# More Strassen products at two levels in three down projections, with the chain's evictions moved from ScalarE and GpSimd to VectorE

## The chip, the cores and the metric

The kernel runs on one core of a Trainium2 chip. The metric is the device time of one execution in microseconds (us); lower is better. The engines are called by the profile's names: PE (TensorE, matmuls; PEld is its weight load), DVE (VectorE), ACT (ScalarE), POOL (GpSimd) and SP (SyncE, which issues the DMAs).

## The reference

Four blocks work on x (2048 tokens by 1024), each with a layernorm before it and a residual sum: a linear attention block (A), a gated bilinear block (B), A again, B again. The change touches B alone:

```python
def _B_ref(x, w_gate, w_up, w_down):
    g = jnp.einsum("bsd,df->bsf", x, w_gate)
    u = jnp.einsum("bsd,df->bsf", x, w_up)
    h = g * u
    return jnp.einsum("bsf,fd->bsd", h, w_down)
...
x = x + _B_ref(_layernorm(x, axis=-1), B_w_gate, B_w_up, B_w_down)
```

Here f is 3584, in 28 tiles of 128. Inputs and output are bf16.

## The kernel before

A B block (`layer_B`) runs over two halves of the tokens (`ps_` 0 and 1). For each half it makes h (`gateup`) and then multiplies it with w_down (`down`). So there are four down stages, called D1 to D4 here: D1 and D2 for the first B block (`first` true, halves 0 and 1), D3 and D4 for the second.

h is kept as four quarters `hA` to `hD` (two token blocks by two halves of f). A down stage uses Strassen's method in Winograd's form: seven products, in the order of `DPROD`, instead of eight. A product of one level is 4 token tiles of 14 matmuls of 128x512 (56). The products listed in `DTWO` are split once more (`two_level`): seven part products, each over 7 of f's tiles, in the order 1, 5, 6, 7, 2, 3, 4, each for p = 0 and 1, as 7 matmuls of 128x256 (98 in all). The part products are put together in PSUM: ACT copies (`seed`) and DVE adds (`join`) between the banks `tmp[p]` and the result banks `dst`. A part product writes to a bank only after the copies and adds that read it are through, since `_Prog.add` orders all accesses of one bank by different engines.

In D2, D3 and D4 (`chain`) products 1, 6 and 7 are summed in the same four PSUM banks: after product 1, after 6 and after 7 the running sum is taken out for each of the four token tiles t (`chain_step`): ACT copies it with a scale to a float32 buffer `rtmp` and POOL adds the residual tile x to it (`evict_x`, L2159 and L2161). Beside that, DVE makes the sums of h that later products need: in step 1 `e = a - d` and `a = c - e`, in step 6 `a = b - a` and `d = d + c`, each over 14 x 128 elements; and `a_sums` makes the four sums of blocks for the next two-level product (7 x 256 elements each), queued in `EX` and taken out one by one by `ex_pop`. The last of these tiles x are brought back from `x_scratch` by DMAs that `tail` issues in the middle of the first token tile of a down stage.

Each engine runs its own stream in the order in which the code calls `P.add`; `plan` turns the dependencies into semaphore waits. There is no scheduler beside it: what stands behind a waiting instruction on its engine waits too. Weights go through a ring of five slots (`ring_issue`); sums of weights for two-level products are made once in D1 (`r_sums`), stored to `d_scratch`, and loaded in D2 to D4. `x_pop` takes from a list of DVE operations that make the sums of x for the next gate and up stage.

L854 and L857 are the helpers `tt` (tensor plus or minus tensor) and `stt` (PSUM by a scale plus a tensor).

## Time and profile before

| | |
|---|---|
| median of 3 runs | 1426.22 us (1425.93 to 1427.45) |
| the profiled execution | 1425.98 us, of which the span is 1424.2 us |
| PE busy | 1419.1 us of the span, 8430 matmuls |
| DVE, ACT, POOL busy | 1167.1, 725.8, 291.1 us |
| D1, D2, D3, D4 | 399 to 483.5, 641 to 725, 1103 to 1184.5, 1342.5 to 1424.2 us |

The span is the time from the first to the last instruction that was recorded. The time of a run is 1.8 us longer than the span in the profiled execution. A busy PE may still have matmuls that follow each other at any pace; the count of matmuls beside the busy time tells the pace. The mean duration of a matmul includes the way through the array, which overlaps with the next one.

### The profile page before, as it was taken

The page shows a single profiled execution, that of the slowest core. Times are in us where ns is not written, and L with a number is a line of the kernel's source. Part 1 is how long each engine was busy: PE and PEld are TensorE (multiplying, and loading weights), DVE is VectorE, ACT ScalarE, POOL GpSimd, SP SyncE. Part 2 cuts the span into 40 slices and gives each one's busy share as a digit, 9 for nine tenths or more (in the row PEclk, how much of TensorE's full clock was granted, in tenths as well). Part 3 has the DMA queues.
Part 4 walks back from the last instruction along what each step waited for, and adds up shares of the span by engine and source line. Part 5 has one row for each costly group of instructions (what it writes and reads, how often), then busy time and mean ns, then how long its engine had stood idle before and what let it go on. Part 6 is the DMA issues. An engine that isn't in the chain of part 4 may idle for free.

```text
span 1424.2 us, 22547 instructions
## 1 busy us (share of the span) xinstructions
PE 1419.1 (100%) x8430; PEld 815.1 (57%) x8430; DVE 1167.1 (82%) x2040; ACT 725.8 (51%) x1529; POOL 291.1 (20%) x303
## 2 busy tenths in 40 slices
PE   9999999999999999999999999999999999999999
PEld 4444444555544655554864444456666477666658
DVE  7878788988878799778778878789877978777887
ACT  4752357667720355552256523557776115777521
POOL 4643632000000000004234346301000400000050
PEclk9999999999999999999999999999999999999999
DMA  7416767988977999996998067589975699778657
GB/s 238 110 23 197 173 139 196 319 285 271 326 249 252 313 270 294 296 255 221 311 335 215 27 180 171 127 230 269 287 257 197 231 319 299 257 259 260 214 189 258
DMA packets 362845, 331.73 MB, mean 233 GB/s; under 512 B 178544, under 2 KB 305776, under 8 KB 362224
## 3 DMA queue, kind: packets, MB, share of 16 engines
q1 hardware_dynamic: 362736, 330.29, 76.7%
q8 instruction: 66, 1.08, 0.3%
q14 instruction: 43, 0.35, 0.1%
HBM read 239.27 MB, written 67.37 MB: 215 GB/s over the span
## 4 chain that ended last, share of the span: by engine, by line
PE 99%; DVE 0%; DMA 0%; ACT 0%; issue 0%; POOL 0%
PE ps L1613 27%; PE ps L1692 18%; PE ps L2208 14%; PE ps L2100 9%; PE ps L1516 8%; PE ps L1414 8%; PE ps L1174 6%; PE ps L980 5%; PE ps L990 3%; PE ps L1428 1%; PE ps L1456 0%; DMA arena<-in_A_x_dram 0%; PE ps L612 0%; DVE arena L487 0%; PE ps L604 0%; PE ps L1440 0%
## 5 line engine op out<-in xcount | busy, mean ns | idle before, releaser
L854 DVE TENSOR_TENSOR arena<-arena 128x512 f16<-128x512 f16 (+9 forms) x784 | 473.5, 632 | 71.4 <-ACT arena L1736 41.2
L1613 PE MATMUL ps<-arena 128*128 128x512 f16 x1808 | 446.8, 380 | 0.0
L1692 PE MATMUL ps<-arena 128*128 128x256 f16 x2324 | 312.4, 273 | 0.7 <-ACT arena L1718 0.6
L857 DVE SCALAR_TENSOR_TENSOR arena<-ps,arena 128x512 f16<-128x512 f32 (+3 forms) x398 | 263.0, 682 | 40.0 <-PE ps L2208 17.9
L1692 PEld LDWEIGHTS ps<-arena 128*128 128x128 f16 (+1 forms) x2324 | 226.8, 98 | 102.1 <-DVE ps L1711 3.2
L1613 PEld LDWEIGHTS ps<-arena 128*128 128x128 f16 (+1 forms) x1808 | 176.8, 98 | 140.5 <-ACT ps L1643 0.3
L2208 PE MATMUL ps<-arena 128*128 128x512 f16 (+1 forms) x896 | 194.2, 380 | 0.0
L1618 ACT ACTIVATE arena<-ps 128x512 f16<-128x512 f32 x220 | 131.6, 598 | 93.1 <-PE ps L1613 91.2
L2161 POOL TENSOR_TENSOR arena<-arena 128x512 f32<-128x512 f32 x44 | 66.0, 1506 | 425.1 <-ACT arena L2159 340.6
L2208 PEld LDWEIGHTS ps<-arena 128*128 128x128 f16 x896 | 87.7, 98 | 105.3
L2100 PE MATMUL ps<-arena 128*128 128x256 f16 (+1 forms) x1176 | 130.1, 273 | 0.0
L2100 PEld LDWEIGHTS ps<-arena 128*128 128x128 f16 x1176 | 114.5, 98 | 14.9 <-DVE arena L857 0.2
L1711 DVE TENSOR_TENSOR ps<-ps,arena 128x256 f32<-128x256 f32 x220 | 92.3, 428 | 30.6 <-PE ps L1692 17.8
L1414 PE MATMUL ps<-arena 128*128 128x512 bf16 x512 | 115.4, 380 | 0.0
L490 POOL TENSOR_SCALAR arena<-arena 128x1 f32<-128x1 f32 x41 | 15.6, 379 | 486.7 <-DVE arena L489 486.7
L1516 PE MATMUL ps<-arena 128*128 128x512 bf16 x512 | 111.5, 380 | 0.0
L1708 ACT COPY ps<-ps 128x256 f32<-128x256 f32 x220 | 81.0, 368 | 48.3 <-PE ps L1692 42.7
L1174 PE MATMUL ps<-arena 128*128 128x512 bf16 (+1 forms) x420 | 94.9, 380 | 0.0
L1314 POOL TENSOR_TENSOR arena<-arena 128x1024 f16<-128x1024 f32 x32 | 80.2, 2506 | 66.4 <-DVE arena L1312 59.3
L1643 ACT COPY ps<-ps 128x512 f32<-128x512 f32 x112 | 64.3, 574 | 51.0 <-PE ps L1692 44.6
L1015 POOL TENSOR_TENSOR arena<-arena 128x512 f32<-128x512 f32 x60 | 73.6, 1245 | 72.2 <-DVE arena L1103 36.2
L1516 PEld LDWEIGHTS ps<-arena 128*128 128x128 f16 x512 | 50.1, 98 | 59.8
(83 smaller groups left out, 1275.5 us busy)
## 6 DMA issues: line engine op xcount, KB each, us to landing
arena<-w_scratch SPq DMA_DIRECT2D x84, 512.0 KB, 4.9
arena<-sp_scratch SPq DMA_DIRECT2D x56, 512.0 KB, 5.8
arena<-t_scratch SPq DMA_DIRECT2D x27, 896.0 KB, 5.7
arena<-in_B_w_down_dram SPq DMA_DIRECT2D x18, 896.0 KB, 6.6
w_scratch<-arena SPq DMA_DIRECT2D x28, 512.0 KB, 6.5
sp_scratch<-arena SPq DMA_DIRECT2D x28, 512.0 KB, 4.1
arena<-in_B_w_gate_dram SPq DMA_DIRECT2D x42, 256.0 KB, 5.0
arena<-in_B_w_up_dram SPq DMA_DIRECT2D x42, 256.0 KB, 3.2
```

Of the source, the lines that this page charges most:

```text
L854: P.add("dve", lambda e: e.tensor_tensor(out=out, in0=a, in1=b, op=op), rd=rd, wr=wr, prd=prd)
L857: P.add("dve", lambda e: e.scalar_tensor_tensor(out=out, in0=a, scalar=sc, in1=b, op0=ALU.mult, op1=op1), rd=rd, wr=wr, prd=prd)
L1174: P.add("pe", lambda e: [e.matmul(psb(bank), x[:, k, :], w[:, k, :], start=(start and k == 0), stop=(k == 3), skip_group_check=True) for k ...
L1414: return [e.matmul(psb(bank), xr[:, t, j * 128:(j + 1) * 128], pk[:, h, t, :], start=(t == tok[0]), stop=(t == tok[-1])) for t in ts]
L1516: return [e.matmul(psb(bank), xnT[:, g, i * 128:(i + 1) * 128], wp[:, g, dh * 512:(dh + 1) * 512], start=(dh == 0 and g == 0), stop=(g == ...
L1613: P.add("pe", lambda e: [e.matmul(psb(bank), w[:, k, :], x[:, k, :], start=(start and k == 0), stop=(k == 3), skip_group_check=True) for k ...
L1618: P.add("act", lambda e: e.activation(t, psb(bank), AF.Copy, scale=SG), prd=[bank], wr=r)
L1692: P.add("pe", lambda e: [e.matmul(psb(bank)[:, 256 * half:256 * half + 256], w[:, k, :], xx[:, k, :], start=(start and k == 0), stop=(k == ...
L1708: P.add("act", lambda e: e.copy(psb(dst[c])[:, 0:256], lo), prd=[bk], pwr=[dst[c]])
L1711: P.add("dve", lambda e: e.tensor_tensor(out=psb(dst[c])[:, 256:512], in0=lo, in1=c5, op=ALU.add), prd=[bk], rd=rc5, pwr=[dst[c]])
L2100: P.add("pe", lambda e: [e.matmul(psb(bank)[:, 256 * half:256 * half + 256], a[:, k, :], w[:, k, :], start=(start and k == 0), stop=(k == ...
L2208: return [e.matmul(psb(bank), hv[:, 7 * hf + k, t * 128:(t + 1) * 128], w[:, k, :], start=(start and hf == 0 and k == 0), stop=(hf == 1 an ...
```

## The change

Two-level products: D2 and D4 have five instead of four (7 is new), D3 has four instead of three (4 is new, and its order becomes that of D2 and D4). So 3 products of 56 matmuls become 3 of 98 half as wide.

In the chain, DVE now takes the running sum out of PSUM with one `stt` that adds x at once; the ACT copies and the POOL adds are gone. Where 7 is two-level, ACT copies the running sum after product 6 to `rtmp` 12 to 15, and the parts of product 7 are added to it by DVE (`ujoin`, `u5`, `ulow`), in place of `seed` and `join`. The sums of step 1 are made the other way round, and `d = d + c` is made in the gate and up stages, once for each of the 14 column blocks of a half. In D1 the sums of weights for 7 are added to the work of product 6 and stored. The `x_pop` calls move from the first products of D1 to its last, and are spread over D3 anew; the stores of x (`stash`) move from steps 6 and 7 to 1 and 6.

```diff
-        L2D = "5324"
-        DPROD = {(True, 0): "1267453", (True, 1): "1672453", (False, 0): "1674253", (False, 1): "1672453"}
-        DTWO = {(True, 0): "", (True, 1): L2D, (False, 0): "532", (False, 1): L2D}
+        L2D = "53247"
+        DPROD = {(True, 0): "1267453", (True, 1): "1672453", (False, 0): "1672453", (False, 1): "1672453"}
+        DTWO = {(True, 0): "", (True, 1): "53247", (False, 0): "5324", (False, 1): "53247"}
...
                 def fmul(q, c):
...
+                    if c and q in "43":
+                        made.append(q)
+                        if len(made) == 2:
+                            j = units[0]["j"]
+                            rc_, rd_ = [R(H[i][1] + j * 1024, 1024) for i in "43"]
+                            tt(hD[:, j, :], hD[:, j, :], hC[:, j, :], ALU.add, rd_ + rc_, rd_)
...
+                def evict7(t, bank):
+                    evict_x(12 + t, bank, xq(1, 0, t))
+                    evict_x(8 + t, bank, xq(1, 1, t))
...
+                    def ujoin(p, b, c):
+                        u, ru = rtmp[12 + p][:, 256 * c:256 * c + 256], R(o_rt[12 + p] + 1024 * c, 1024)
+                        P.add("dve", lambda e: e.tensor_tensor(out=psb(b)[:, 256 * c:256 * c + 256], in0=psb(tmp[p])[:, 0:256], in1=u, op=ALU.add),
+                              prd=[tmp[p]], rd=ru, pwr=[b])
+                    def u5(p):
+                        v, rv = u_pair(p)
+                        P.add("dve", lambda e: e.tensor_tensor(out=v, in0=two(p, 1), in1=v, op=ALU.add), prd=[tmp[p]], rd=rv, wr=rv)
+                    def ulow(p, b):
+                        u = rtmp[14 + p].rearrange("p (c x) -> p c x", c=2)
+                        P.add("dve", lambda e: e.tensor_tensor(out=psb(b).rearrange("p (c x) -> p c x", c=2), in0=two(p, 0), in1=u, op=ALU.add),
+                              prd=[tmp[p]], rd=rr(14 + p), pwr=[b])
...
                             if i == 1:
                                 mm(1, p, tmp[p], 0, True)
-                                seed(p, hi)
+                                ujoin(p, hi, 0) if q == "7" else seed(p, hi)
                             elif i == 5:
                                 mm(5, p, tmp[p], 1, False)
+                                if q == "7":
+                                    u5(p)
+                                    continue
...
                             elif i == 6:
                                 mm(6, p, tmp[p], 0, False)
-                                join(p, hi)
+                                ujoin(p, hi, 1) if q == "7" else join(p, hi)
...
                                 mm(7, p, tmp[p], 0, False)
+                                if q == "7":
+                                    ulow(p, lo)
+                                    continue
...
-                def evict_x(t, bank, k, *xs):
-                    P.add("act", lambda e: e.activation(rtmp[k], psb(bank), AF.Copy, scale=CD), prd=[bank], wr=rr(k))
-                    for k2, (x, rx) in xs:
-                        P.add("pool", (lambda k2, x: lambda e: e.tensor_tensor(out=rtmp[k2], in0=rtmp[k], in1=x, op=ALU.add))(k2, x), rd=rx + rr(k), wr=rr(k2))
+                def evict_x(k, bank, x):
+                    stt(rtmp[k], psb(bank), CD, x[0], x[1], rr(k), prd=[bank])
...
                     if q == "1":
-                        tt(e_, a, d, ALU.subtract, r[0] + r[3], r[4])
-                        evict_x(t, bank, t, (t, xq(0, 0, t)))
-                        tt(a, c, e_, ALU.subtract, r[2] + r[4], r[0])
+                        evict_x(t, bank, xq(0, 0, t))
+                        tt(a, d, a, ALU.subtract, r[3] + r[0], r[0])
+                        tt(e_, c, a, ALU.subtract, r[2] + r[0], r[4])
                     elif q == "6":
-                        evict_x(t, bank, 4 + t, (4 + t, xq(0, 1, t)))
+                        evict_x(4 + t, bank, xq(0, 1, t))
+                        if "7" in l2d:
+                            P.add("act", lambda e: e.copy(rtmp[12 + t], psb(bank)), prd=[bank], wr=rr(12 + t))
                         tt(a, b, a, ALU.subtract, r[0] + r[1], r[0])
-                        tt(d, d, c, ALU.add, r[3] + r[2], r[3])
+                        ex_pop(1)
                     elif q == "7":
-                        evict_x(t, bank, 8 + t, *([(12 + t, xq(1, 0, t))] if four else []), (8 + t, xq(1, 1, t)))
+                        if four:
+                            evict_x(12 + t, bank, xq(1, 0, t))
+                        evict_x(8 + t, bank, xq(1, 1, t))
                         ex_pop(1)
...
-                    if q == "7" and chain:
-                        EX.extend(a_sums("2"))
+                    if chain and q == ("6" if "7" in l2d else "7"):
+                        EX.extend(a_sums("7" if q == "6" else "2"))
...
-                    x_pop({"4": [2, 2, 2, 2], "5": [0, 0, 0, 1], "3": [1, 3, 0, 2]}[q][t])
+                if first and q in "453":
+                    x_pop({"4": [1, 1, 1, 0], "5": [1, 1, 1, 0], "3": [2, 2, 2, 2]}[q][t])
+                elif not first and q in "2453":
+                    x_pop({"2": [0, 1, 0, 1], "4": [0, 1, 0, 1], "5": [0, 0, 0, 0], "3": [3, 3, 3, 3]}[q][t])
```

In the rows below a name such as `s_pe` is the semaphore of an engine, and `d_x8` that of the DMA which brings tile 8 of x. `128x14x128` is a sum for one token tile, `128x7x256` one of `a_sums`.

The first place is the start of D2. Before, DVE passes from the last multiplications of the gate and up stage to the sums of the first token tile, which wait for PE and DVE:

```order
L854 TENSOR_TENSOR arena<-arena 128x512 [waits s_dve]
L857 SCALAR_TENSOR_TENSOR arena<-ps,arena 128x512 [waits s_act,s_pe]
L854 TENSOR_TENSOR arena<-arena 128x14x128 [waits d_spw531,s_dve]
L854 TENSOR_TENSOR arena<-arena 128x14x128 [waits s_pe,s_dve]
L854 TENSOR_TENSOR arena<-arena 128x14x128
```

POOL's additions of x, which wait for the DMAs of the x tiles, stand in its own stream there (those of steps 1 and 6):

```order
L2161 TENSOR_TENSOR arena<-arena 128x512 [waits d_x8,s_act]
L2161 TENSOR_TENSOR arena<-arena 128x512 [waits d_x9,s_act]
L2161 TENSOR_TENSOR arena<-arena 128x512 [waits d_x10,s_act]
L2161 TENSOR_TENSOR arena<-arena 128x512 [waits d_x11,s_act]
L2161 TENSOR_TENSOR arena<-arena 128x512 [waits s_act] x4
```

With the change DVE's stream has, for the first three token tiles of product 1:

```order
L854 SCALAR_TENSOR_TENSOR arena<-ps,arena 128x512 [waits d_spw531,d_x8,s_pe]
L851 TENSOR_TENSOR arena<-arena 128x14x128 [waits s_dve] x2
L854 SCALAR_TENSOR_TENSOR arena<-ps,arena 128x512 [waits d_x9,s_pe]
L851 TENSOR_TENSOR arena<-arena 128x14x128
L851 TENSOR_TENSOR arena<-arena 128x14x128 [waits s_dve]
L854 SCALAR_TENSOR_TENSOR arena<-ps,arena 128x512 [waits d_x10,s_pe]
```

So the wait for the x tiles has moved from POOL to DVE, with DVE's sums behind it.

The second place is DVE between product 6 and the next two-level product, in D4. Before, that is the end of product 6, product 7 at one level (its four `128x7x256` rows) and the start of product 2:

```order
L854 TENSOR_TENSOR arena<-arena 128x14x128 [waits s_pe]
L854 TENSOR_TENSOR arena<-arena 128x14x128
L854 TENSOR_TENSOR arena<-arena 128x7x256
L854 TENSOR_TENSOR arena<-arena 128x7x256 [waits s_dve] x2
L854 TENSOR_TENSOR arena<-arena 128x7x256
L854 TENSOR_TENSOR arena<-arena 128x1792 [waits s_pe]
L2107 TENSOR_TENSOR ps<-ps,arena 128x256 [waits s_pe] x2
```

With the change, the last token tile of product 6 (first three rows) and product 7 at two levels up to its first eviction:

```order
L854 SCALAR_TENSOR_TENSOR arena<-ps,arena 128x512 [waits s_pe]
L851 TENSOR_TENSOR arena<-arena 128x14x128
L851 TENSOR_TENSOR arena<-arena 128x7x256
L2123 TENSOR_TENSOR ps<-ps,arena 128x256 [waits s_act,s_pe] x2
L851 TENSOR_TENSOR arena<-arena 128x7x256
L2128 TENSOR_TENSOR arena<-ps,arena 128x2x256 [waits s_act,s_pe] x2
L2123 TENSOR_TENSOR ps<-ps,arena 128x256 [waits s_pe] x2
L851 TENSOR_TENSOR arena<-arena 128x7x256
L2132 TENSOR_TENSOR ps<-ps,arena 128x512 [waits s_pe] x2
L851 TENSOR_TENSOR arena<-arena 128x7x256 [waits s_dve]
L851 TENSOR_TENSOR arena<-arena 128x7x256
L854 SCALAR_TENSOR_TENSOR arena<-ps,arena 128x512 [waits d_x12,s_pe]
```

L2123 is `ujoin`, L2128 `u5`, L2132 `ulow` in the changed file. The two-level product that used to follow a whole one-level product now stands right behind product 6, and its first part sums are on DVE instead of ACT.

85 lines of the change are left out of this document (41 added, 44 removed).

## The prediction

> **What bounds the kernel now.** I read the page's busy times and its chain first.
>
> ```profile
> PE 1419.1 (100%) x8430; PEld 815.1 (57%) x8430; DVE 1167.1 (82%) x2040; ACT 725.8 (51%) x1529; POOL 291.1 (20%) x303
> PE 99%; DVE 0%; DMA 0%; ACT 0%; issue 0%; POOL 0%
> ```
>
> PE carries the whole chain, so each us of matmul that goes is a us of time, and each us in which PE is made to wait comes back in full. The table by stage shows how much room the other engines have (columns: stretch, length, busy PE, PEld, DVE, ACT, POOL, granted clock, DMA):
>
> ```profile
> 236.00:399.00 163.00, 163.00 (x937) 91.41 (x935) 141.80 (x328) 114.45 (x247) 2.47 (x6) 1.00 0.93 304
> 399.00:483.50 84.50, 84.50 (x447) 43.45 (x445) 66.85 (x89) 8.55 (x18) 0.00 (x0) 1.00 0.78 258
> 641.00:725.00 84.00, 84.00 (x585) 56.96 (x584) 65.84 (x77) 19.14 (x42) 26.48 (x19) 1.00 0.81 274
> 1103.00:1184.50 81.50, 81.50 (x529) 51.29 (x527) 65.69 (x79) 14.69 (x33) 16.60 (x12) 1.00 0.83 279
> 1184.50:1342.50 158.00, 157.66 (x1114) 108.52 (x1113) 122.38 (x243) 113.78 (x289) 0.00 (x0) 1.00 0.77 251
> 1342.50:1424.20 81.70, 79.27 (x562) 54.59 (x560) 65.64 (x76) 15.85 (x36) 23.93 (x16) 1.00 0.69 234
> ```
>
> In D1 to D4 (second, third, fourth and last row) DVE is busy four fifths of the time, ACT a fifth; the change takes work from the idle engines to the full one. D4's groups of instructions and its DVE forms price the parts:
>
> ```profile
> L2100 PE MATMUL ps<-arena 128*128 128x256 f16 (+1 forms) x392 | 43.0, 273 | 0.0
> L2208 PE MATMUL ps<-arena 128*128 128x512 f16 (+1 forms) x168 | 36.4, 380 | 0.0
> L2161 POOL TENSOR_TENSOR arena<-arena 128x512 f32<-128x512 f32 x16 | 23.9, 1503 | 218.1 <-ACT arena L2159 217.8
> L854 DVE TENSOR_TENSOR arena<-arena 128x1792 f16<-128x1792 f16 x28 | 29.9, 1085 | 1.3 <-PE ps L2208 1.1
> L854 DVE TENSOR_TENSOR arena<-arena 128x1792 f16<-128x1792 f16 x32 | 43.7, 1400 | 0.9 <-PE ps L2208 0.6
> ```
>
> The fourth row is D1, where POOL is idle: a sum of 1792 elements takes 1085 ns. In D4 (fifth row), beside POOL's 16 additions, the same form takes 1400 ns on average. Without POOL I reckon with 1085.
>
> How DVE keeps pace, from the timeline of D4 at product 2 (start, length, what, [idle before]):
>
> ```profile
> 1378.81 12.39 PE L2100 MATMUL ps<-arena 128*128 128x256 bf16 x112
> 1382.83 0.43 DVE L2107 TENSOR_TENSOR ps<-ps,arena 128x256 f32<-128x256 f32 x1 [4.00 <-PE ps L2100]
> 1383.60 0.43 DVE L2107 TENSOR_TENSOR ps<-ps,arena 128x256 f32<-128x256 f32 x1 [0.33 <-PE ps L2100]
> 1383.94 1.08 DVE L854 TENSOR_TENSOR arena<-arena 128x1792 f16<-128x1792 f16 x1
> 1385.86 2.08 DVE L854 TENSOR_TENSOR arena<-arena 128x1792 f16<-128x1792 f16 x2
> 1387.86 2.55 DVE L857 SCALAR_TENSOR_TENSOR arena<-ps,arena 128x512 bf16<-128x512 f32 x4
> ```
>
> DVE starts product 2 with 4.00 us of idle behind it, so the join comes as soon as its matmuls are through: 4.02 us after the product's start, where 35 matmuls take 35 x 43.0 / 392 = 3.84; the way from PE to DVE is 0.18. From start to start a sum of 1792 costs 2.08 - 1.08 = 1.00, an eviction (2.55 - 0.69) / 3 = 0.62, a join 0.34.
>
> **The change part by part.** Matmuls: a one-level product is 56 x 36.4 / 168 = 12.13 us, a two-level one 98 x 43.0 / 392 = 10.75. Three products change: 3 x 1.38 = **4.15 us less**, all of it on the path.
>
> Product 7 at two levels in D4. Step 6 ends with three operations on DVE for its last token tile: eviction, sum, and the fourth of `a_sums`. Both tile budgets hold against PE's 12.13 / 4 = 3.03 per tile: step 1 is 0.62 + 1.12 + 1.00 = 2.74 (the second sum needs the first; three sums in 3.21 in the DVE row of D2 below), step 6 is 2.62. But those last three begin 0.18 after step 6's last matmul, and only behind them stands the first `ujoin`, which the matmuls of part 5 wait for, since they write the bank it reads. It starts at 0.18 + 0.62 + 1.00 + 1.00 = 2.80 and ends at 3.23. Without a wait, part 5 would start after 14 matmuls, at 1.54. PE stands 1.7 us. Before, this first step was an ACT copy, and the two-level product came after a one-level product in which DVE drained.
>
> Then one more of `a_sums` stands ahead of `u5`: `ujoin` again from 3.14, the sum from 3.48, `u5` from 4.48 to 5.17 (0.69, as an eviction of 512 elements), while part 6, which writes the bank that `u5` reads, could start at 3.23 + 1.54 = 4.77: 0.4 more. The rest of product 7 on DVE (two `ujoin`, two `ulow`, three sums, eight evictions) starts when part 6's first matmuls are through, at 5.17 + 0.77 + 0.18 = 6.1, and is about 0.7 + 1.2 + 3.0 + 5.0 = 9.9 us long, to 16.0, while PE ends the product at 10.75 + 1.7 + 0.4 = 12.9. Product 2's first sum lasts to 17.0, and its join, due at 12.9 + 4.02 = 16.9, is late by a little: I take 0.3. D4 loses **2.4 us** to waits, against the 1.38 that it gains. Both ends: 0, if DVE were through with step 6 in time, and 5.0, if `u5` and `ulow`, which no row shows, took twice the eviction's time (four operations, 0.62 each more).
>
> D2 has the same 2.4, and a wait of its own, since the first eviction now waits for tile x8:
>
> ```profile
> 640.57 1.68 PE L2208 MATMUL ps<-arena 128*128 128x512 bf16 x7
> 647.48 14.84 PE L2208 MATMUL ps<-arena 128*128 128x512 bf16 x68
> 648.04 4.36 SPq L447 DMA_DIRECT2D arena<-x_scratch  x8
> 654.68 1.15 POOL L2161 TENSOR_TENSOR arena<-arena 128x512 f32<-128x512 f32 x1 [83.12 <-DMA arena<-x_scratch]
> 656.57 5.15 POOL L2161 TENSOR_TENSOR arena<-arena 128x512 f32<-128x512 f32 x3 [0.73 <-DMA arena<-x_scratch]
> 648.49 3.21 DVE L854 TENSOR_TENSOR arena<-arena 128x1792 f16<-128x1792 f16 x3
> ```
>
> The first half tile of product 1 runs at 640.57, the rest from 647.48. The x tiles are issued at 648.04, and POOL's first addition starts at 654.68, released by that DMA; DVE meanwhile made its sums from 648.49 on. The same kilobytes stand ahead of x8 in SP's queue after the change (half of a weight unit is merely fetched from another tensor), so I take 654.68 for DVE's first eviction. Behind it stand four tiles of 2.74 and four of 2.62: 21.4 us, up to 676.1, with `ujoin` to 676.6. PE ends step 6 at 647.48 + 1.52 + 3 x 3.03 + 12.13 = 670.2 and would start part 5 at 671.8. That is a wait of 4.8 instead of 1.7; with 0.4 and 0.3 behind it D2 loses **5.5 us**. Ends: 2.4 (x8 lands before DVE needs it, at 649.2) and 7.4 (x8 as late as x9 was, 656.57 - 654.68 = 1.9 more). POOL's own row is the nearest, so 5.5.
>
> In D4 the tiles x11 to x15 are the only ones to come back, and x11 is needed at the fourth tile; D3 is alike. I cost them at nothing: 12.13 us of product 1 cover it, where D2's first tile needed 654.68 - 648.04 = 6.6 from issue.
>
> D3 gets product 4 at two levels, which is built as before (ACT copies), so no `ujoin`. Product 7 stays one-level, with DVE at two evictions and a sum per tile, 2.24 of 3.03. What can be late are the sums for the next gate and up stage, two of which move into product 2 and two into product 4:
>
> ```profile
> L854 DVE TENSOR_TENSOR arena<-arena 128x2048 f16<-128x2048 f16 x4 | 4.9, 1215 | 0.0
> ```
>
> The first stands ahead of product 2's evictions. They would end near 9.7 (first eviction, 1387.86 - 1378.81 + 0.69), 1.0 before product 4 starts and writes the same bank; with 1.2 added they are 0.2 late, and the joins of the next products may be late by as much: **0.5**, between 0 and 2 x 1.2.
>
> D1: the sums of weights for 7 replace `d = d + c` in step 6, a 1792 sum for a 1792 sum; of two `x_pop` that lengthen the last products, the last join is late by **0.2** (0 to 1.2). Their three stores wait on SP for nothing that PE needs.
>
> The `d = d + c` of the gate and up stages: 4 x 14 sums of 512, with 0.42 us each in D4's preceding stage, 23.5 us of DVE in all, in stages where it idles (163 - 141.8) / 14 = 1.5 to (158 - 122.4) / 14 = 2.5 us for each column block.
>
> ```profile
> L854 DVE TENSOR_TENSOR arena<-arena 128x512 f16<-128x512 f16 x75 | 31.5, 424 | 26.9 <-ACT arena L1736 25.5
> PEld ps L1692 <- DVE ps L1711: 3.2, 20, 0.2
> ```
>
> Most of that idle time is a wait for ACT, which the new sum fills. PE already waits 20 times for a join of DVE, 0.2 us at most. If all 20 came later by the sum's 0.42 it were 8.4 us; 0 if the idle time takes all. I take **0.7**, near the lower end, since the idle is at least 3.5 times the sum.
>
> The POOL additions and ACT copies that go were on no path (POOL waited 217.8 us before them): nothing. The stores of x that move ahead in SP's queue, 256 KB each, stand before weights that are needed a product later: nothing, covered by that product's 12 us.
>
> Sum, against the profiled execution: 1425.98 - 4.15 + 5.5 + 2.4 + 0.5 + 0.2 + 0.7 = **1431.1 us**. Its own time lies 0.24 under the median of the runs, which I leave uncorrected. A change of less than 0.2% (2.9 us) can't be told from none.
>
> **Rivals.** A: the clock falls. At the start of the program, PE comes from idle:
>
> ```profile
> L990 PE MATMUL ps<-arena 128*128 128x512 bf16 x75 | 16.9, 380 | 0.3 <-ACT arena L606 0.3
> L454 PE MATMUL ps<-arena 128*128 128x512 f16 x10 | 4.5, 632 | 1.4 <-POOL arena L450 1.4
> 0.00:4.00 4.00, 2.64 (x7) 0.99 (x8) 0.93 (x2) 1.28 (x1) 2.61 (x20) 1.00 0.46 125
> ```
>
> The first ten matmuls take 632 ns instead of 380: 10 x 0.252 = 2.5 us lost before the pace is reached. If the 4.8 us of standstill in D2 bring PE back to that state, the time is 1433.6. No wait of before is long enough to show it. [...]
>
> B: x8 comes in time, because the DMA queue has less ahead of it than I think. Then D2 loses 2.4 and the time is 1425.98 - 4.15 + 2.4 + 2.4 + 0.5 + 0.2 + 0.7 = 1428.0, no measurable change. Against it speaks POOL's start at 654.68.
>
> C: the matmuls of part 5 don't meet a late `ujoin`: faster. It needs DVE at most 1.54 - 0.18 - 0.43 = 0.9 us behind PE at the end of step 6 instead of 2.6 (beyond that every us costs a us in D2 and D4). The mean of 1400 ns that falls to 1085 without POOL speaks for it, DVE's idle time in sum too; the order, with 2.62 us of work released by the last matmul of step 6, against it. The time would be 1425.98 - 4.15 + 0.5 = 1422.3.
>
> D: the new sums make joins late in all gate and up stages: 8.4 instead of 0.7, so 1438.8. Their idle time speaks against it.
>
> **How the numbers follow.** The forecast has 0.50, its own range 1429.1 to 1433; A 0.14, B 0.16, C 0.15, D 0.05. Range: leaving out C and D (0.20) it goes from B with the costs of D1, D3 and the gate and up stages at nothing, 1425.98 - 4.15 + 4.8 = 1426.6, to A with D3 and D1 at their upper ends, 1433.6 + 1.9 + 1.0 = 1436.5. Faster is C with a little of B: 0.16. Same is most of B and the forecast's lower tail: 0.17. Slower is the rest: 0.67.
>
> **What would show it.** In the profile after: PE busy falls by about 4 us, and the first idle time on PE in a down stage appears at L2109 (the part products), released by DVE's `ujoin` (L2123), near 4.8 us once in D2 and 1.7 in D4, then 0.4 by L2128. DVE waits in D2 some 5 us for `x_scratch`; its 1792 sums take 1085 throughout D2 and D4. D3 is shorter by about 0.9. Wrong would be the forecast if PE shows no gap at L2109 (C), if D2's gap is like D4's (B), or if idle time shows at L1688, the gate and up stage's part products (D); a matmul mean well above 380 right after D2's gap is A.

## The result, and the profile after

The changed kernel takes 1435.69 us (median of six runs, 1434.28 to 1437.31), the kernel before 1426.84 beside it (1425.91 to 1428.70): a ratio of 1.0064, 95% interval 1.0053 to 1.0075. It is slower by 8.85 us, and 4.6 above the predicted 1431.1. The profiled execution of the changed kernel took 1437.31, the longest of the six.

Busy times and the chain first:

```profile
PE 1418.1 (99%) x8502; PEld 828.1 (58%) x8556; DVE 1196.6 (83%) x2164; ACT 711.2 (50%) x1507; POOL 224.5 (16%) x259
PE 93%; DVE 4%; DMA 1%; issue 1%; ACT 0%; SPq 0%; POOL 0%; DVEq 0%; ACTq 0%
```

The chain, which was PE alone before (99%), now runs through DVE for 4% of the span: PE waits for it. (54 of the 8556 matmul records are missing; the weight loads are complete.) The table by stage, with D1, D2, D3 and D4 in this order:

```profile
400.90:486.50 85.60, 84.31 (x442) 43.11 (x443) 66.65 (x88) 8.47 (x18) 0.00 (x0) 1.00 0.86 282
644.40:735.40 91.00, 86.14 (x626) 62.54 (x628) 70.63 (x103) 14.67 (x34) 1.03 (x3) 0.96 0.81 271
1113.50:1194.40 80.90, 79.97 (x567) 55.14 (x567) 67.36 (x98) 9.70 (x27) 0.00 (x0) 1.00 0.85 290
1352.80:1435.50 82.70, 78.11 (x601) 58.34 (x600) 69.16 (x101) 11.04 (x28) 0.00 (x0) 1.00 0.75 247
```

D2 has grown from 84 to 91 us, PE idles there for 4.9, and it is the one stage whose granted clock is not 1.00. The list of waits names the cause, and the timeline of PE in D2 (first two rows) and in D4 (last two) the places:

```profile
PE ps L2109 <- DVE ps L2123: 6.2, 2, 4.6
PE ps L2109 <- DVE ps L2139: 0.8, 1, 0.8
PE ps L2109 <- DMA arena<-d_scratch: 0.8, 1, 0.8
```

```profile
673.79 1.69 PE L2109 MATMUL ps<-arena 128*128 128x256 f16 x14
680.10 16.82 PE L2109 MATMUL ps<-arena 128*128 128x256 f16 x126 [4.62 <-DVE ps L2123]
...
1380.13 1.70 PE L2109 MATMUL ps<-arena 128*128 128x256 f16 x14 [1.60 <-DVE ps L2123]
1382.06 14.14 PE L2109 MATMUL ps<-arena 128*128 128x256 f16 x125 [0.22 <-DVE arena L2128]
```

Part 1 of product 7 runs (14 matmuls), then PE stands 4.62 us in D2 and 1.60 in D4 until DVE has made the first `ujoin` (L2123). In D4 14 matmuls then take 1.70 us. In D2 126 of them take 16.82 us, where 0.109 each would make 13.8. The windows behind D2's wait show why (the number ahead of the DMA share is the granted clock):

```profile
681.00:682.00 1.00, 1.00 (x7) 0.67 (x5) 0.56 (x2) 0.00 (x0) 0.00 (x0) 0.50 0.00 0
684.00:686.00 2.00, 2.00 (x11) 1.39 (x10) 0.43 (x1) 0.00 (x0) 0.00 (x0) 0.50 0.85 219
```

For 28 matmuls the clock is halved: they start every 0.213 us instead of 0.109, which is 2.89 us lost behind the 4.62.

Lengths of the stages, worked out from the weight loads, since in eight of these traces the record of a stage's first matmul is among the missing ones (us). D is counted from its first weight load to its last, D2 to the first of the attention stage; G is the gate and up stage ahead of a down stage. The attention stage and G3 together last 378.1 in all of them (378.3 in e11) and are left out.

| kernel | G1 | D1 | G2 | D2 | D3 | G4 | D4 |
|---|---|---|---|---|---|---|---|
| before | 163.3 | 84.4 | 157.1 | 84.6 | 81.4 | 158.0 | 79.0 |
| after | 163.6 | 85.9 | 157.6 | 91.2 | 81.1 | 158.2 | 80.1 |
| e1, evictions held in D2 | 164.4 | 85.9 | 157.6 | 85.7 | 80.3 | 158.2 | 80.1 |
| e3, product 7 at one level | 164.0 | 85.9 | 157.5 | 90.5 | 81.0 | 158.2 | 79.0 |
| e4, gate and up sums alone | 163.9 | 84.4 | 157.1 | 84.6 | 81.4 | 158.0 | 79.0 |
| e5, step 6's sums put off | 163.6 | 85.9 | 157.5 | 88.5 | 80.3 | 158.3 | 78.3 |
| e6, e1 and e5 | 164.1 | 85.9 | 157.6 | 83.8 | 80.3 | 158.3 | 78.4 |
| e7, D1 and D3 | 164.4 | 85.1 | 157.5 | 89.8 | 80.3 | 158.2 | 80.1 |
| e8, e6 and e7 | 164.2 | 85.1 | 157.5 | 83.8 | 80.3 | 158.3 | 78.6 |
| e9, PE kept busy | 163.6 | 85.9 | 157.6 | 89.0 | 80.3 | 158.2 | 80.1 |
| e10, D3 alone | 163.7 | 84.4 | 157.1 | 84.6 | 80.3 | 158.2 | 79.0 |
| e11, e8 and D1 again | 164.1 | 84.4 | 157.2 | 83.8 | 80.3 | 158.3 | 78.3 |
| e12, e11 and a later sum | 163.6 | 84.4 | 157.2 | 84.4 | 80.3 | 158.3 | 78.9 |

G1 is no part of the result: in e10, which is the kernel before up to D3, it took 163.7 as well. The profiled execution of after also spent 1.4 us more ahead of G1 than that of before. That time changes from execution to execution (0 to 0.2 more in e5, e6, e7 and e9, 2.6 in e4, which has the same code there), so it is left out too.

An idle time in the rows starts at the end of a matmul's record, 0.27 us after its start, while the next could have started 0.11 after it. So a wait ahead of a 128x256 matmul costs PE 0.16 us more than the idle time that the row gives.

### The profile page after: what moved, and what is told of

It reads as the page before. It is cut to its first block, busy times and chain, and to the rows that moved or that the text cites. A ratio compares the mean times of both kernels' runs of the same rounds, so it can differ in the third digit from the quotient of the medians.

```text
span 1435.5 us, 22773 instructions
## 1 busy us (share of the span) xinstructions
PE 1418.1 (99%) x8502; PEld 828.1 (58%) x8556; DVE 1196.6 (83%) x2164; ACT 711.2 (50%) x1507; POOL 224.5 (16%) x259
## 4 chain that ended last, share of the span: by engine, by line
PE 93%; DVE 4%; DMA 1%; issue 1%; ACT 0%; SPq 0%; POOL 0%; DVEq 0%; ACTq 0%
PE ps L1609 27%; PE ps L1688 18%; PE ps L2246 9%; PE ps L2109 8%; PE ps L1512 8%; PE ps L1410 8%; PE ps L1170 6%; PE ps L976 5%; PE ps L986 3%; DVE arena L851 2%; DVE arena L854 1%; DMA arena<-d_scratch 1%; PE ps L1424 1%; PE ps L1452 0%; DMA arena<-x_scratch 0%
## 5 line engine op out<-in xcount | busy, mean ns | idle before, releaser
L851 DVE TENSOR_TENSOR arena<-arena 128x512 f16<-128x512 f16 (+8 forms) x840 | 470.1, 584 | 61.0 <-ACT arena L1732 31.1
L854 DVE SCALAR_TENSOR_TENSOR arena<-ps,arena 128x512 f16<-128x512 f32 (+3 forms) x446 | 294.1, 683 | 46.0 <-PE ps L2246 18.6
L2109 PE MATMUL ps<-arena 128*128 128x256 f16 (+1 forms) x1470 | 166.4, 275 | 8.4 <-DVE ps L2123 6.2
L2109 PEld LDWEIGHTS ps<-arena 128*128 128x128 f16 x1470 | 144.1, 99 | 29.9 <-DVE ps L2123 6.8
L2246 PE MATMUL ps<-arena 128*128 128x512 f16 (+1 forms) x719 | 156.8, 379 | 0.5
L2246 PEld LDWEIGHTS ps<-arena 128*128 128x128 f16 x728 | 71.3, 98 | 85.4
L2136 ACT COPY ps<-ps 128x256 f32<-128x256 f32 x52 | 18.6, 357 | 185.1 <-PE ps L2109 184.6
L1704 ACT COPY ps<-ps 128x256 f32<-128x256 f32 x220 | 80.9, 368 | 51.3 <-PE ps L1688 43.5
L1170 PE MATMUL ps<-arena 128*128 128x512 f16 (+1 forms) x411 | 94.4, 379 | 0.5
L1011 POOL TENSOR_TENSOR arena<-arena 128x512 f32<-128x512 f32 x60 | 73.7, 1246 | 72.2 <-DVE arena L1099 36.1
L1512 PEld LDWEIGHTS ps<-arena 128*128 128x128 f16 x512 | 50.1, 98 | 59.8
```

Source lines behind the costliest of these rows:

```text
L851: P.add("dve", lambda e: e.tensor_tensor(out=out, in0=a, in1=b, op=op), rd=rd, wr=wr, prd=prd)
L854: P.add("dve", lambda e: e.scalar_tensor_tensor(out=out, in0=a, scalar=sc, in1=b, op0=ALU.mult, op1=op1), rd=rd, wr=wr, prd=prd)
L1170: P.add("pe", lambda e: [e.matmul(psb(bank), x[:, k, :], w[:, k, :], start=(start and k == 0), stop=(k == 3), skip_group_check=True) for k ...
L1512: return [e.matmul(psb(bank), xnT[:, g, i * 128:(i + 1) * 128], wp[:, g, dh * 512:(dh + 1) * 512], start=(dh == 0 and g == 0), stop=(g == ...
L1704: P.add("act", lambda e: e.copy(psb(dst[c])[:, 0:256], lo), prd=[bk], pwr=[dst[c]])
L2109: P.add("pe", lambda e: [e.matmul(psb(bank)[:, 256 * half:256 * half + 256], a[:, k, :], w[:, k, :], start=(start and k == 0), stop=(k == ...
```

## Experiments

Each was run in turns with the kernel before; differences are between medians of the same set of runs. After stands 8.85 above before.

**e1: D2's evictions held back.** In D2 each eviction of step 1 comes two token tiles later on DVE (the last two behind the last sums), so DVE makes sums while the tiles are on their way:

```diff
+                held = []
...
                     if q == "1":
-                        evict_x(t, bank, xq(0, 0, t))
+                        held.append((t, bank, xq(0, 0, t)))
+                        if not first or t > 1:
+                            evict_x(*held.pop(0))
                         tt(a, d, a, ALU.subtract, r[3] + r[0], r[0])
                         tt(e_, c, a, ALU.subtract, r[2] + r[0], r[4])
+                        while t == 3 and held:
+                            evict_x(*held.pop(0))
```

> The kernel after, with one change in D2 alone: in step 1 of product 7's left operands the DVE eviction of tile 0 is held back by two tiles and that of tile 1 by two as well, so DVE makes its sums first and nothing on it stands behind the late tile x8. Nothing else moves. My theory: the 4.62 us standstill ahead of part 5 comes from DVE's first eviction waiting for x8, with 21 us of DVE work queued behind it; D2's wait falls to that of D4 (1.60 us), which is 3.0 us less, and because PE no longer stands still for 4.6 us the half clock after it (28 matmuls at 213 instead of 109 ns, 2.9 us) goes too: 5.9 us less, about 1429.8. Rival 1 (the clock's fall has nothing to do with the standstill's length): 3.0 less, 1432.7, with the slow matmuls still there. Rival 2 (DVE is late because of its amount of work, not of x8): no change, 1435.7, and the same gap near 4.6 us.

1430.38, 4.22 above before (ratio 1.0029, 1.0018 to 1.0040), so 4.6 less than after, where 5.9 was forecast. First DVE in D2 as after has it, then as e1 has it, then PE in e1 and a window behind the wait:

```profile
658.30 0.69 DVE L854 SCALAR_TENSOR_TENSOR arena<-ps,arena 128x512 f32<-128x512 f32 x1 [5.63 <-DMA arena<-x_scratch]
```

```profile
653.87 2.22 DVE L851 TENSOR_TENSOR arena<-arena 128x1792 f16<-128x1792 f16 x2 [0.16 <-PE ps L2252]
656.89 2.22 DVE L851 TENSOR_TENSOR arena<-arena 128x1792 f16<-128x1792 f16 x2 [0.80 <-PE ps L2252]
660.07 0.69 DVE L854 SCALAR_TENSOR_TENSOR arena<-ps,arena 128x512 f32<-128x512 f32 x1 [0.96 <-DMA arena<-x_scratch]
...
678.11 1.70 PE L2109 MATMUL ps<-arena 128*128 128x256 f16 x14 [1.60 <-DVE ps L2123]
680.04 2.14 PE L2109 MATMUL ps<-arena 128*128 128x256 f16 x18 [0.22 <-DVE arena L2128]
```

```profile
678.00:680.00 2.00, 1.70 (x14) 1.29 (x14) 2.00 (x5) 0.00 (x0) 0.00 (x0) 1.00 0.91 286
```

In after DVE idles 5.63 us for the tile; in e1 it works in most of that time and idles 0.96. D2's wait becomes D4's to the hundredth (1.60 and 0.22), and the clock stays at 1.00. D2 is 5.5 us shorter. The tile is the cause of the longer wait; rival 2 is out. Whether the clock falls because of the wait's length needs a run in which PE doesn't stand although DVE is late: e2 and e9.

**e2: 20 matmuls in the gap.** A list of 20 matmuls of 128x512 on `hE` (`hv`) and `hB`, ahead of part 5:

```diff
+                            if i == 5 and q == "7" and first and not p:
+                                P.add("pe", lambda e: [e.matmul(psb(0), hv[:, k % 7, 0:128], hB[:, k % 7, :], start=True, stop=True) for k in range(20)], ...)
```

> The kernel after, with 20 more matmuls of 128x512 in D2 just ahead of part 5 of product 7, where PE now stands still. They go into a free bank and are thrown away, so this kernel does more work than the one after: 20 x 0.217 = 4.3 us of PE at a place where PE waited 4.62 us for DVE's first ujoin. DVE's work is as before, so part 5 starts at about the same time. Theory (the standstill lets TensorE's clock fall, which costs 2.9 us after it): no standstill above 1 us is left, the matmuls behind it run at 109 ns from the start, the granted clock stays at 1.00, and the time falls by 2.9 to 1432.8 although 20 matmuls were added. Rival (the slow matmuls are a property of the place, such as contention on the bank or on memory, and not of the standstill): they remain at 213 ns and the time stays at 1435.7 or rises a little.

1440.69, 14.53 above before (1.0104, 1.0090 to 1.0117). The run can't decide what it was built for:

```profile
678.93 6.18 PE L2146 MATMUL ps<-arena 128*128 128x512 f16 x20 [4.54 <-DVE arena L851]
```

The added matmuls read h that a sum on DVE was still writing, so PE stood 4.54 us ahead of them, and then ran them as well, the first eight at 0.427 us each. It says nothing for the rival: these are other instructions, in another bank, and slow behind a standstill of the same length.

**e9: 42 matmuls that wait for nothing.** Part 1's own operands, read once more into a free bank:

```diff
+                            if i == 5 and q == "7" and first and not p:
+                                for _ in range(6):
+                                    mm(1, 0, 0, 0, True)
```

> The kernel after, with 42 more matmuls of 128x256 in D2 just ahead of part 5 of product 7: six times the seven matmuls of part 1, on operands that part 1 has just read, into a free bank, thrown away. Unlike the 20 of the run before, they wait for nothing. They take 42 x 0.109 = 4.6 us, the length of the standstill, and DVE's work is as before. Theory (the length of the standstill lets TensorE's clock fall): PE runs through, the clock stays at 1.00, the matmuls of parts 5 and on run at 109 ns, and with 42 matmuls more the time is 2.9 us less than after's 1435.7, 1432.8, or ratio 1.0044. Rival (the slow matmuls belong to the place): 1435.7, the same slow stretch behind the added matmuls.

1434.01, 7.89 above before (1.0054, 1.0042 to 1.0067). The timeline of PE and the windows:

```profile
672.47 6.28 PE L2109 MATMUL ps<-arena 128*128 128x256 f16 x56
679.13 1.70 PE L2109 MATMUL ps<-arena 128*128 128x256 f16 x14 [0.39 <-DVE ps L2123]
681.05 11.20 PE L2109 MATMUL ps<-arena 128*128 128x256 f16 x101 [0.22 <-DVE arena L2128]
```

```profile
676.00:680.00 4.00, 3.61 (x34) 3.01 (x32) 4.00 (x7) 0.59 (x1) 0.00 (x0) 1.00 0.78 270
680.00:684.00 4.00, 3.78 (x35) 3.12 (x34) 3.23 (x6) 0.00 (x0) 0.00 (x0) 1.00 0.54 156
```

DVE is as late as before, PE works through, and no slow matmul is left: part 5's 14 take 1.70 us. With 42 matmuls more, D2 is 2.2 us shorter (91.2 to 89.0). So in D2 it is behind the standstill that the clock halves (0.50 in after, 1.00 here), and this costs 2.2 net, since u5's 0.22 and 0.39 at the `ujoin` were covered before. In the medians the gain is 1.0 where 2.9 were forecast, and the two intervals overlap: the trace shows it, the times alone would not. One reason is that the slow stretch is not always as long: in e7, whose D2 is that of after, it is half (14 matmuls, 1.43 us); see the last section. The mean granted clock of the runs agrees with the trace: it is below 1.00 in all six of after (0.998 or 0.999) and 1.000 in four of the five of e9.

**e3: product 7 back at one level in D2 and D4.**

```diff
-        DTWO = {(True, 0): "", (True, 1): "53247", (False, 0): "5324", (False, 1): "53247"}
+        DTWO = {(True, 0): "", (True, 1): "5324", (False, 0): "5324", (False, 1): "5324"}
```

> The kernel after, with product 7 back at one level in D2 and D4 (five products at two levels become four there; product 4 in D3 at two levels, the sums in the gate and up stages and DVE's evictions in place of ACT's and POOL's stay). The matmul gain of 2 x 1.38 us is given back. My theory: with it go both ujoin waits (4.62 in D2, 1.60 in D4), the 2.9 us of slow matmuls, u5's 0.22, so the net is +2.76 - 9.3 = -6.6, about 1429; a remainder of the D2 loss may stay at product 2's join. Rival (the loss in D2 is made by moving the evictions to DVE, whatever product 7 is): the waits come back at product 2's joins and the time stays within 2 us of 1435.7.

1432.22, 6.06 above before (1.0045, 1.0033 to 1.0058), where about 1429 was forecast; a miss. With one level, product 7 takes two slots fewer of the weight ring, and D2's last product then shares slots with weights that are loaded for the next stage (`in_A_wqkv`). So part of it is multiplied with those weights: the time is that of the full work, but the result isn't the block's. That brought a wait of its own (timeline, then a window behind it):

```profile
725.37 8.83 PE L2109 MATMUL ps<-arena 128*128 128x256 f16 x64 [4.13 <-DMA arena<-in_A_wqkv_dram]
```

```profile
726.00:728.00 2.00, 2.00 (x11) 1.43 (x10) 0.43 (x1) 0.00 (x0) 0.00 (x0) 0.50 1.10 367
```

Two things can still be read. After a standstill for a DMA, too, the clock falls to 0.50 (16 slow matmuls, 1.65 us). And D4, which has no such trouble, takes 79.0 us, as before: with the chain's evictions on DVE but product 7 at one level there is neither gain nor loss. So the loss is not made by moving the evictions alone; it is made where `ujoin` meets them.

**e5: `ujoin` first.** The `a` sums of step 6's last two tiles go into products 2 and 4:

```diff
-                        tt(a, b, a, ALU.subtract, r[0] + r[1], r[0])
-                        ex_pop(1)
+                        if "7" in l2d and t > 1:
+                            later.append(lambda: tt(a, b, a, ALU.subtract, r[0] + r[1], r[0]))
+                            ex_pop(2 if t == 2 else 0)
+                        else:
+                            tt(a, b, a, ALU.subtract, r[0] + r[1], r[0])
+                            ex_pop(1)
...
+                        if "7" in l2d and q in "72":
+                            ex_pop({6: 1, 7: 2, 2: 1}.get(i, 0))
...
+                        if later and (q == "2" and i == 4 or q == "4" and i == 2):
+                            later.pop(0)()
```

> The kernel after, with DVE's work at the end of step 6 put off where product 7 has two levels: the `a` sums of the last two token tiles move into products 2 and 4, and the weight sums are popped early, so that behind step 6's last matmul only one eviction stands ahead of the first ujoin instead of an eviction and two sums. Nothing is left out. Theory (the ujoin waits because two sums of about 1 us stand ahead of it): D4's gap at L2109 goes from 1.60 to about 0 (1.3 net, since product 2's join may be late by up to 0.6), D2's from 4.62 to about 2.6, which is too short for the clock to fall (2.9 more): 1.3 + 2.0 + 2.9 = 6.2 less, about 1429.5; 1432.4 if the clock still falls at a gap of 2.6. Rival (DVE's total is what counts, so that each sum postponed comes back at product 2's joins): 1434 to 1436, with the gaps moved to L2139.

1429.91, 3.83 above before (1.0025, 1.0015 to 1.0035). D4 fell from 80.1 to 78.3: both waits at product 7 are gone, and 0.26 at product 2's first join stands in their place. In D2 (timeline, then a window behind the wait):

```profile
677.34 12.88 PE L2109 MATMUL ps<-arena 128*128 128x256 f16 x102 [3.16 <-DVE ps L2123]
```

```profile
678.00:680.00 2.00, 2.00 (x11) 1.45 (x10) 0.69 (x1) 0.00 (x0) 0.00 (x0) 0.50 0.56 216
```

The time is 5.0 less than after, where 6.2 was forecast: the wait is 3.16 instead of 2.6, and behind it the clock fell in the profiled run (14 slow matmuls, 1.38 us). That 2.6 is too short for a fall was the author's estimate; no run has a wait of that length there. The clock doesn't fall in every run: four of the eight have a mean clock of 1.000 and took 1428.79 to 1429.39, four have 0.999 and took 1430.44 to 1432.10. Of the postponed sums no more than that 0.26 came back at product 2, so the rival is out.

**e6: e1 and e5 together.**

> The kernel after with both: evictions of step 1 held in D2 so that DVE doesn't wait for x8, and two sums of step 6 put off. Theory (two separate causes, one wait each): no ujoin gap above 0.5 us in D2 or D4 and no fall of the clock: 1435.7 - 4.6 - 2.9 - 1.3 + 0.6 = 1427.5, where the time stands beside before's 1426.8 only through what D1, D3 and the gate and up stages cost. Rival (both act on the same slack, so that the second adds nothing): equal to the better of the two alone, about 1429.5.

1426.75, 0.67 above before (1.0003, 0.9994 to 1.0012). All idle time of PE at L2109 is now 1.5 us, more than half of it in D1 and none at `ujoin`:

```profile
L2109 PE MATMUL ps<-arena 128*128 128x256 f16 (+1 forms) x1470 | 163.4, 273 | 1.5 <-DVE ps L2139 1.4
```

D2 and D4 are 0.8 and 0.7 shorter than before. The two waits have two causes, and each goes alone.

**e4: the sums of the gate and up stages alone**, put into the kernel before, with `d = d + c` taken out of the down stages (step 1's sums as in after):

```diff
+                    if c and q in "43":
+                        made.append(q)
+                        if len(made) == 2:
+                            ...
+                            tt(hD[:, j, :], hD[:, j, :], hC[:, j, :], ALU.add, rd_ + rc_, rd_)
...
-                        tt(d, d, c, ALU.add, r[3] + r[2], r[3])
...
-                            tt(hd, hd, hc, ALU.add, rd_ + rc, rd_)
```

> The kernel BEFORE, with only one part of the change: the sum d = d + c that product 3 reads is taken out of the down stages' first steps and made in the gate and up stages (56 DVE sums of 128x512 added there), with the first sums of step 1 in the order that the kernel after has. All products stay as they were. It prices the term of 0.7 us. My forecast of 0.7 gives 1427.5 (joins a little later in the gate and up stages). The stages' lengths in the trace of after point to 1.7: 1428.5. Rival D of the prediction (every join later by the sum's 0.42): 8.4, 1435.2. If DVE's relief in the down stages matters: below 1426.8.

1426.91, 0.75 above before (1.0006, 0.9997 to 1.0015). G2, G4 and all down stages are as before to 0.1 us. The list of waits has one of 0.2 more than before's (second row; the first stands before too):

```profile
PE ps L1692 <- ACT arena L1718: 0.6, 2, 0.3
PE ps L1692 <- DVE arena L854: 0.2, 1, 0.2
```

Rival D (8.4) is out; the 56 sums cost nothing that these runs can tell from zero.

**e7: D1 and D3.**

```diff
-                if q == "4" and t < 2 and not first:
+                if q == "7" and t < 2 and not first:
                     sp_load(1, t, "12")
...
-                    x_pop({"4": [1, 1, 1, 0], "5": [1, 1, 1, 0], "3": [2, 2, 2, 2]}[q][t])
+                    x_pop({"4": [1, 1, 1, 1], "5": [1, 1, 1, 1], "3": [0, 2, 2, 2]}[q][t])
```

> The kernel after with two small moves in D1 and D3 and D2 and D4 left alone. In D1 the sums of 2048 for the next stage are spread one to a tile over products 4 and 5, so that none stands ahead of the first joins of product 3; in D3 the loads of the 512 KB tiles are issued in product 7 instead of product 4, where they stand ahead of the load that product 2 or 3 waits for. Theory: D1's 0.85 us gap (join, L2139) and its 0.3 at the next stage's start go, and D3's 0.76 us gap (released by the DMA of d_scratch): 1.9 less, 1433.8. Rival (the gaps are replaced by like ones at the next place: the DMA queue has as much to carry): within 0.5 of 1435.7.

1434.00, 7.92 above before (1.0053, 1.0039 to 1.0066), so 0.9 less than after, where 1.9 was forecast. DVE at the start of D1's last product, and PE behind it, in after and then DVE in e7:

```profile
476.14 2.35 DVE L851 TENSOR_TENSOR arena<-arena 128x2048 f16<-128x2048 f16 x2
478.41 0.76 DVE L2139 TENSOR_TENSOR ps<-ps,arena 128x256 f32<-128x256 f32 x2
478.89 3.23 PE L2109 MATMUL ps<-arena 128*128 128x256 f16 x28 [0.85 <-DVE ps L2139]
```

```profile
475.88 1.21 DVE L851 TENSOR_TENSOR arena<-arena 128x2048 f16<-128x2048 f16 x1
477.01 0.93 DVE L2139 TENSOR_TENSOR ps<-ps,arena 128x256 f32<-128x256 f32 x2
```

One sum of 2048 instead of two stands ahead of the joins, and D1 is 0.8 shorter. For D3 the run shows nothing: its 0.76 us wait for `d_scratch` is gone, but it is gone as well in e1, e5, e6 and e9, which load at the same place as after. It comes and goes with the transfers, not with the order.

**e8: all four moves.**

> The kernel after with all four moves: evictions of D2's step 1 held, step 6's sums put off, D1's sums spread, D3's loads issued later. No operation is removed or added. Theory (all losses are waits made by the order of work on DVE and in the queue, apart from what the gate and up sums cost): 1427.5 - 1.9 = 1425.6, which is not above before's 1426.8, so that the matmul gain of 4.15 us is nearly used up by 1 to 2 us in the gate and up stages and by small waits. Rival (the amount of DVE work is the bound): 1429 or more with waits at L2139.

1425.90, 0.18 below before (0.9997, 0.9988 to 1.0006). The loss of 8.85 us is undone by order alone, with no operation taken out: it was waits, not the amount of DVE's work.

**e10: D3 alone.** The kernel before with product 4 of D3 at two levels:

```diff
-        DPROD = {..., (False, 0): "1674253", ...}
-        DTWO = {..., (False, 0): "532", ...}
+        DPROD = {..., (False, 0): "1672453", ...}
+        DTWO = {..., (False, 0): L2D, ...}
...
```

> The kernel BEFORE, with one part of the change alone: product 4 of D3 at two levels (with the order 1, 6, 7, 2, 4, 5, 3 there, the sums for the next stage at after's places, and the loads of the 512 KB tiles in product 7). D1, D2, D4, the evictions and the sums of the gate and up stages stay as before. Theory (each two-level product saves 1.38 us of matmul, and D3 showed 1.3 to 1.4 of it wherever no DMA wait stood in it; what eats the gain elsewhere is product 7 and its sums in D1): D3 80.3 instead of 81.6, 1426.1 - 1.3 = 1424.8, ratio 0.9991. Rival (the waits in the stages behind D3 come from D3's fuller DVE): the stage after D3 longer by 0.4, so 1425.2 or no change.

1425.95, 0.17 below before (0.9999, 0.9990 to 1.0007). D3 gives 1.1 (81.4 to 80.3), and G4 takes 0.2 back, half of what the rival has; what is left is too small for the medians to show. The 1.1 is the 1.38 of the matmuls less two small waits: the first matmul of product 4 starts 0.33 instead of 0.11 after the one ahead of it, held by DVE's evictions of product 2, and one in product 3 starts 0.27 after.

**e11: D1's sums further forward.** On top of e8:

```diff
-                    x_pop({"4": [1, 1, 1, 1], "5": [1, 1, 1, 1], "3": [0, 2, 2, 2]}[q][t])
+                    x_pop({"4": [1, 4, 0, 1], "5": [1, 1, 1, 1], "3": [0, 1, 1, 2]}[q][t])
```

> The kernel of the four moves together, with one more: in D1 the sums for the next stage are brought forward into product 4's second tile, where DVE stood idle for 1.0 us, so that the last of the sums of 2048 comes about 1 us earlier. Nothing is added or removed. Theory (D1 and the stage behind it are longer than before by 0.4 and 0.7 because DVE ends D1 with work left over): 0.3 to 0.7 less than the 1425.9 of the four moves. Rival (DVE is full from product 5 on, so the left-over work is the same): 1425.9, no change.

1425.01, 1.11 below before (0.9994, 0.9985 to 1.0003). D1 is back at 84.4, G2 at 157.2, together 1.0 less than in e8. It is the shortest of all, though its interval still includes no change.

**e12: product 2's join earlier.** e11 with the third of the sums that product 2 reads moved from product 7 into product 2:

```diff
-                            ex_pop({6: 1, 7: 2, 2: 1}.get(i, 0))
+                            ex_pop({6: 1, 7: 1 + (q == "2"), 2: 1 + (q == "2")}.get(i, 0))
...
-                        ex_pop(8)
+                        ex_pop(0 if q == "2" and "7" in l2d else 8)
...
-                            EX.extend(a_sums(nq))
+                            EX.extend([a_sums(nq)[k] for k in ((0, 1, 3, 2) if q == "7" else (0, 1, 2, 3))])
```

> The kernel of the five moves, with one more in D2 and D4: the third sum of product 2's left operands, which only its part 3 reads, is made behind product 2's joins of part 6 instead of in product 7, where it stands ahead of the eight evictions and so makes product 2's first join late. Nothing is added or removed. Theory (product 2's join waits 0.26 us, 0.43 from step to step, in D2 and in D4 because DVE leaves product 7 late): both waits go, 0.5 to 0.8 less than the 1425.0 of the five moves, 1424.4, ratio 0.9989. Rival (the sum only moves the wait to product 2's next join or its evictions): no change, 1425.0, with the idle time at a later L2139.

1426.36, 0.15 above before (1.0002, 0.9993 to 1.0011). The intervals of e11 and e12 overlap, but in the traces D2 and D4 are 0.6 longer each than in e11. DVE in product 2, and PE:

```profile
688.38 4.34 DVE L851 TENSOR_TENSOR arena<-arena 128x1792 f16<-128x1792 f16 x4
692.63 2.48 DVE L854 SCALAR_TENSOR_TENSOR arena<-ps,arena 128x512 bf16<-128x512 f32 x4
695.02 2.21 DVE L851 TENSOR_TENSOR arena<-arena 128x1792 f16<-128x1792 f16 x2
697.15 0.76 DVE L2139 TENSOR_TENSOR ps<-ps,arena 128x256 f32<-128x256 f32 x2
697.63 2.58 PE L2109 MATMUL ps<-arena 128*128 128x256 f16 x22 [0.85 <-DVE ps L2139]
```

The 0.26 at product 2's join is gone, and 0.85 at product 4's first join stands in its place, in D2 and in D4: DVE has next to no idle time left there, so what is taken from one join falls on the next. Here the rival of e5 and e8, the amount of work, does hold.

## Why the prediction was right or wrong

The direction and the mechanism of the waits held; the size was 3.7 us short of the 8.85. The measured 1435.69 lies above the forecast's own range (1429.1 to 1433), near the end of the whole one (1436.5), which only rival A reaches. By the prediction's steps, with the waits counted from start to start of the matmuls (0.16 more than the idle times):

- Matmuls, -4.15. Held: 56 steps of 0.216 are 12.1 us, 98 of 0.109 are 10.7. No stage keeps all of the 1.38: D3 without a DMA wait gains 1.1 (e10), and D2 and D4 gain 0.8 and 0.7 once their long waits are out (e6), with 0.26 of idle time left at one join.
- D2's wait, 4.8 forecast, 4.8 measured (4.62 of idle time), by the path foretold: DVE idles 5.63 us for x8 (5 forecast) and then has its 21 us of work, up to `ujoin`. e1 shows the tile to be the cause, against rival B. The `ujoin` of after:

```profile
679.62 0.76 DVE L2123 TENSOR_TENSOR ps<-ps,arena 128x256 f32<-128x256 f32 x2
```

- The clock after it (rival A, 0.14). This is the step that failed: the sum put the fall at nothing and gave it a chance of 0.14, and it happened. It is 2.89 us in the trace of after, 2.2 net by e9. The row that bore on it was the slow start, 632 ns for the first ten matmuls, and it was the right row, although the granted clock reads 1.00 there: their step, (4.45 - 0.63) / 9 = 0.424 in the timeline of before, is that of e2's first eight at half clock (0.427). Its 2.5 us is near the 2.89 here and above the 1.4 to 1.7 of e3, e5 and e7. The sign that was named for A, a mean above 380 ns, is of the wrong width: the matmuls behind the gap are of 128x256, and what shows the fall is their step, 0.213 instead of 0.109. The chance of 0.14 was the author's estimate, and no run shows so low a share; PE's longest wait in before is 1.4 us, too far from this one to price it. Of the gaps of 3.16, 4.13, 4.54, 4.53 and 4.62 us (e5, e3, e2, e7, after) each one in a profiled run was followed by the fall, and none of 1.60 (D2 in e1, D4 in after, e1, e7 and e9) was; over the timed runs the mean clock is below 1.00 in all eleven of after and e7 and in four of the eight of e5.
- D2's and D4's small waits, 0.4 by `u5` and 0.3 at product 2's join: 0.38 and 0.31 in D4 (0.22 and 0.15 of idle time). In D2 the slow matmuls covered the first.
- D4, 1.7 forecast, 1.76 measured (1.60 of idle time); its length +1.0 forecast, +1.1 measured. Rival C is out.
- D3, 0.5 forecast for late sums. It held: in e1 and e10 PE loses 0.2 ahead of product 4, where product 2's evictions are late, and 0.2 in product 3. Beside that, in the profile of after, a load of `d_scratch` was 0.76 late, by chance, and the fuller DVE costs 0.2 in G4 (e10), which the step didn't look at.
- D1, 0.2 forecast, 1.5 measured, and 0.5 more in G2. The term was mis-sized: it counted one sum of 1.2 ahead of the last join with most of it hidden, and there were two (2.35 us), with DVE full from product 5 on. e7 takes back 0.8 of D1, e11 all 1.5 and 0.3 of G2.
- The gate and up sums, 0.7 forecast. e4 measured 0.75, with 0 inside its interval and one new wait of 0.2 in the trace, and its stages behind G1 are as before: it is not shown that they cost anything. Rival D is out.
- Sums of 1792 at 1085 ns without POOL. Held: in D4, where the mean was 1400, DVE's forms now read

```profile
L851 DVE TENSOR_TENSOR arena<-arena 128x1792 f16<-128x1792 f16 x32 | 34.0, 1084 | 0.1
L2123 DVE TENSOR_TENSOR ps<-ps,arena 128x256 f32<-128x256 f32 x4 | 1.6, 429 | 0.8 <-PE ps L2109 0.8
L2132 DVE TENSOR_TENSOR ps<-ps,arena 128x512 f32<-128x512 f32 x2 | 1.3, 692 | 0.0
L2128 DVE TENSOR_TENSOR arena<-ps,arena 128x512 f32<-128x512 f32 x2 | 1.3, 682 | 0.0
```

So in the trace of after D2 cost 2.5 more than forecast (+6.6 instead of +4.1), D1 and G2 1.8 more, D3 and G4 0.7 more (the late load among it), D4 0.1 more, and the gate and up sums 0.7 less: 4.4, against the 3.7 in the medians. That execution was 1.6 above the median of its six; the rest is not resolved.

## What to carry to other kernels

When work moves from a stage's idle engines to its busy one, look first at what that engine has queued ahead of the next operation that PE needs, and at what the head of its queue waits for: here this order cost 8.85 us net, and the same work in another order nothing. A wait of PE can cost more than its length: here 1.4 to 2.9 us more, in half of the runs where the profile has a wait of 3.2 us, in all where it has 4.5 or 4.6, and in none of e1, where it has 1.6. So a forecast of a wait of this length should carry the clock's fall in its sum and not as a rare rival. Where the engine is full, moving one sum only moves the wait (e12).

## What the runs showed of the hardware that was not expected

The fall of the clock comes in two sizes. Behind waits of 3.16, 4.13 and 4.53 us, 14 to 16 matmuls of 128x256 ran at half speed (1.38 to 1.65 us lost, e5, e3, e7); behind 4.62 us in after it were 28 (2.89). The windows of e7 behind its wait, which ended at 678.60:

```profile
680.00:682.00 2.00, 2.00 (x13) 1.46 (x12) 0.92 (x2) 0.00 (x0) 0.00 (x0) 0.61 0.02 7
682.00:684.00 2.00, 1.98 (x19) 1.51 (x17) 1.40 (x4) 0.00 (x0) 0.00 (x0) 1.00 0.65 165
```

In e7 full speed is back within 3.4 us of the wait's end, where after still read 0.50 between 684 and 686, 3.9 to 5.9 us after its own. The same D2 ran in e7 and in after, so the stretch isn't set by the wait's length alone.

The granted clock of narrower windows gives the length of the half speed: 3.4 us in e2, e3, e5 and e7, and 6.8 in after (679.24 to 686.06). In e2 and e3 the clock fell only behind the wait's end; in e7, e5 and after it fell 0.44, 0.56 and 0.86 us ahead of it, and after has the longest half speed. Five traces are read here, and no run tests what sets the length.

A mean clock of 0.998 for a whole run, which looks like nothing, is 2.9 us here. It takes the trace to place it: 0.999 came in 10 of the 74 runs of e1, e4, e6, e8 and e10 to e12 as well, which have no such wait in a down stage. In the profile of e4, one of the ten, the matmuls of L990, most of them in the program's first 45 us, take 386 ns on average instead of 380 in before, with a wait of 2.0 us for a DMA; no other group's mean is more than 1 ns above that of before.
